# Decay attention and two gated MLPs: at most three loads of SyncE's queue under way

## The chip, the core and the metric
The kernel runs on one core of a Trainium2 chip. The metric is the device time of one execution in microseconds. Three runs of the kernel before took 586.87 us in the median (585.73 to 587.20). The engines are named as in the profile: PE (TensorE), PEld (its weight loads), DVE (VectorE), ACT (ScalarE), POOL (GpSimd) and SP (SyncE, which here issues all loads and stores).

## The reference
Batch 2, 8 heads, 768 positions, 64 channels per head; then 1536 tokens of 512 channels.

```python
for b in range(nb):                       # blocks of 64 positions
    intra = (qb @ kb.T * Dmask) @ vb      # Dmask: powers of the head's lam, lower triangle
    inter = (qb * lam_pow) @ kv_state
    out[:, :, sl] = intra + inter
    kv_state = lam_block * kv_state + (kb * rev_pow).T @ vb
x = out as tokens x 512
x = (sigmoid(x @ w_gate) * (x @ w_val)) @ w_out            # d_ff 1536
h = x @ w_in;  out = where(h > 0, h, exp(min(h, 0)) - 1) @ w_out2   # d_ff 2048
```

## The kernel before, in words
The attention takes the sequence in six chunks of 128 positions (`NCH`). For chunk c the kernel loads `tin` (k and q with channels on partitions; "t" of `load`, two halves of 512 KB for chunks 0 to 2, one load of 1 MB for the others) and `nat` (k and v with positions on partitions; "k" and "v", 512 KB each). `scores(c)` multiplies k and q (tile `st`, read from `tin`), in two halves g; behind each half it multiplies the decayed k of the chunk before with v (also into the bank of `st`, read from `nat` and `kd`; called u here). DVE masks the scores into `pr`, the x products multiply `pr` with v, and the ql product adds what the state `sn` brings. `split_chunk` splits the result into a high and a low part for the matmuls in fp32r, each dense product being three matmuls.

The first gate and value weights of the first MLP are multiplied directly while the attention runs (`direct`, tiles that the profile calls `warm` and `direct` by the name of their bank). All later products of a weight group go over seven fast products (M1 to M7, a scheme that saves one product of eight) with sums of weights made by POOL and DVE. A weight group is loaded raw into one buffer `w64` of 1 MB; ACT and DVE restore the floats from it (`fetch`), so the next raw group can be loaded when DVE's last step has read the buffer. The out products accumulate 256 columns of d_ff at a time in `xu`.

Nothing is issued where it is written. All operations are recorded as `Op`, `hazards` finds which wait for which, and `run` plays them through with costs for each engine, a list scheduler that is tried with several rules; `issue` then emits the instructions in the order of the best of these plays. So each engine runs its own fixed list, and a new edge in the graph can move any instruction of any engine but keeps the dependences. For SP, `hazards` chains the DMAs in the order in which the program writes them, and `run` treats the successor in this chain as ready once SP has issued the DMA before, not once it has landed. An `Op` can have a `fence`: another operation for which its first instruction waits by a dependence made by hand (`add_manual_dep`). Before the change only the ql product has one.

All operations are issued from one line of the helper, L182 in the profile, so its rows are told apart by tiles.

Of the kernel before, what the change touches and what calls it, by code (L numbers as in the profile page):

```python
# [108 lines left out]


class Op:
    __slots__ = ("eng", "call", "reads", "writes", "gap", "took", "port", "table", "preds", "shape", "fence", "words")

    def __init__(self):
        self.fence, self.words = None, 0


class Engine:
# [9 lines left out]
class Work:  # L128
# [78 lines left out]
    def hazards(self):  # L207
        write, read, banks, tables = {}, {}, {}, {1: [], 2: []}
        holder, users, freed = {}, {}, {}
        queued = -1  # L210
        for k, op in enumerate(list(self.ops)):
            e = ENGINES.index(op.eng)
            before = set()
            for v in op.reads + op.writes:
                slot = v.buf.slot
                if holder.setdefault(slot, v.buf) is not v.buf:
                    holder[slot] = v.buf
                    gone = Op()
                    gone.eng, gone.call, gone.preds = None, lambda: None, sorted(users.pop(slot))
                    freed[slot] = len(self.ops)  # L220
                    self.ops.append(gone)
                users.setdefault(slot, set()).add(k)
                if slot in freed:
                    before.add(freed[slot])
            for views, writes in ((op.reads, False), (op.writes, True)):
                for v in views:
                    for h in v.halves:
                        at = (v.buf.slot, h)
                        if v.buf.psum:
                            by = banks.setdefault(at, ({}, []))  # L230
                            before.update(by[0].values())
                            before.update(x for f, x in by[1] if writes or f != e)
                            continue
                        if at not in write:
                            write[at] = np.full(WORDS, -1, np.int32)
                            read[at] = []
                        before.update(np.unique(write[at][v.ix]).tolist())
                        if writes:
                            before.update(x for x, words in read[at] if words[v.ix].any())
            for views, writes in ((op.reads, False), (op.writes, True)):  # L240
                for v in views:
                    for h in v.halves:
                        at = (v.buf.slot, h)
                        if v.buf.psum:
                            if writes:
                                banks[at] = ({e: k}, [])
                            else:
                                banks[at][1].append((e, k))
                        elif writes:
                            write[at][v.ix] = k  # L250
                            for x, words in read[at]:
                                words[v.ix] = False
                            read[at] = [r for r in read[at] if r[1].any()]
                        else:
                            words = np.zeros(WORDS, bool)
                            words[v.ix] = True
                            read[at].append((k, words))
            if op.table:
                before.update(tables[3 - op.table])
                tables[op.table].append(k)  # L260
            if op.fence:
                before.add(self.ops.index(op.fence))
            if op.eng == "sync":
                before.add(queued)
                queued = k
            before -= {-1, k}
            op.preds = sorted(before)

    def run(self, preds, key, backward=False, gate=None, stick=0, thrift=20000):
        ops = self.ops[::-1] if backward else self.ops  # L270
        n = len(ops)
# [6 lines left out]
        free = dict.fromkeys(ENGINES, 0.0)  # L278
        port = behind = 0.0
# [23 lines left out]
        for _ in range(sum(op.eng is not None for op in ops)):  # L303
            t, e = min((free[e] if ripe[e] else max(free[e], soon[e][0][0]), i, e)
                       for i, e in enumerate(ENGINES) if ripe[e] or soon[e])[::2]
            while soon[e] and soon[e][0][0] <= t:
                k = heapq.heappop(soon[e])[1]
                heapq.heappush(ripe[e], (key[k], k))
            rank, k = heapq.heappop(ripe[e])
            if e == "tensor" and stick and ops[k].shape != shape:  # L310
                like = min((x for x in ripe[e] if x[0] < rank + stick and ops[x[1]].shape == shape), default=None)
                if like:
                    ripe[e].remove(like)
                    heapq.heapify(ripe[e])
                    heapq.heappush(ripe[e], (rank, k))
                    k = like[1]
            if e == "tensor" and not backward and thrift and stall(ops[k], t) > 100:
                like = min((x for x in ripe[e] if x[0] < rank + thrift and not stall(ops[x[1]], t)), default=None,
                           key=lambda x: (ops[x[1]].words, x))
                if like:  # L320
                    ripe[e].remove(like)
                    heapq.heapify(ripe[e])
                    heapq.heappush(ripe[e], (rank, k))
                    k = like[1]
            op = ops[k]
            if e == "sync":
                late = 300 if queue < t + 2000 or t < 3000 else 1100
                queue = max(t + 2000, queue) + op.took
                free[e], end[k] = t + op.gap, queue + late
            elif e == "tensor":  # L330
                t += 60 if t > free[e] + 1 else 0
                t += self.SWITCH if op.shape != shape else 0
                shape = op.shape
                late = 0.0
                if not backward:
                    late = stall(op, t, True)
                    told += op.words
                free[e], end[k] = t + late + op.gap, t + late + op.took
            else:
                if op.table and op.table != table:  # L340
                    t, table = t + self.TABLE, op.table
                go = max(t, port, behind if e == "gpsimd" else 0) if op.port else t
                free[e], end[k] = go + op.gap, go + op.took
                if op.port:
                    port = free[e]
                    behind = end[k] + self.HANDOFF["gpsimd"] if e == "vector" else 0
            start[k] = t
            done = [k]
            while done:
                x = done.pop()  # L350
                for s in after[x]:
                    f = ops[s].eng
                    ready = free[e] if f == e and e in ("tensor", "sync") and x == k else end[x] + self.HANDOFF.get(f, 0)
                    at[s] = max(at[s], ready)
                    left[s] -= 1
                    if left[s]:
                        continue
                    if f is None:
                        start[s] = end[s] = at[s]
                        done.append(s)  # L360
                    else:
                        heapq.heappush(soon[f], (at[s], s))
# [40 lines left out]
def tile_decay_attention_two_mlps(  # L403
# [245 lines left out]
    def load(c, what="tvk"):  # L649
        if c in tin:  # L650
            pass
        elif c == 2:
            tin[c] = sb.tile([P, 2, 2, 2, 2, CH], F32, "xPh1", name="tin2")
            nat_of[c] = sb.tile([P, 2, 2, H, D], F32, "sig1", name="nat2")
        else:
            tin[c] = sb.tile([P, 2, 2, 2, 2, CH], F32, ("gh1", "gl1")[int(c in (1, 4))], name="tin")
        t = tin[c].rearrange("p g b q i n -> p (g b q i n)"), att[c, 0]
        n = nat_of[c].rearrange("p q b h e -> p (q b h e)"), att[c, 1]
        first, second = slice(0, 1024), slice(1024, 2048)
        for x in what:  # L660
            for (to, src), cols in {"t": ((t, first), (t, second)) if c < 3 else ((t, slice(0, 2048)),), "v": ((n, second),),
                                    "k": ((n, first),)}[x]:
                nc.sync.dma_start(out=to[:, cols], in_=src[:, cols])

    load(0, "tv")
# [27 lines left out]
    n = 1  # L693
# [338 lines left out]
```

## Time and profile before
| | |
|---|---|
| median of three runs | 586.87 us (585.73 to 587.20) |
| the profiled execution's own time | 586.36 us |
| its span, first to last instruction | 584.6 us |
| mean granted clock of PE | 0.997 |
| PE busy | 573.1 us, 98% |
| DVE, ACT, POOL busy | 387.1, 301.7, 312.3 us |
| loads and stores | 51.4 MB, 24.1% of the DMA engines' span |

The span is 1.8 us shorter than the time of the execution, which includes start and end. PE's records are pipelined and a matmul's end is modelled, so its busy share says when matmuls followed one another, not that each was at its best. Idle time of the other engines means little as long as PE has work.

### The profile page before, as it was taken

To read this page: it belongs to the slowest core of one execution; us is meant where nothing else is said; L and a number is where in the kernel's file an instruction comes from. 1 tells how busy PE (TensorE), PEld (TensorE's weight loads), DVE (VectorE), ACT (ScalarE), POOL (GpSimd) and SP (SyncE) were. 2 spreads that over 40 slices of the span, in tenths; PEclk is the share of its full clock that TensorE was granted. 3 is DMA by queue.
4 is the path that set the end of the run, shared out by engine and by line. 5 is a ranking of instruction groups with operands and counts; after the bars stand their busy time and mean duration, and the time that the engine had idled before them with its cause. 6 is when DMAs were issued, how large, how long until landed. Compare 5 with 4: busy or idle time off the path is not lost.

```text
span 584.6 us, 10090 instructions
## 1 busy us (share of the span) xinstructions
PE 573.1 (98%) x4020; PEld 492.1 (84%) x4022; DVE 387.1 (66%) x683; ACT 301.7 (52%) x586; POOL 312.3 (53%) x265
## 2 busy tenths in 40 slices
PE   6999999999999999999999999999999999999997
PEld 3888898888888888888899788888888888888886
DVE  5787753476475466456549975677767685868484
ACT  4794656532433424344147887764545464636160
POOL 0688779567457447567238883572626355461100
PEclk9899999999999999999999999999999999999999
DMA  8955212321111201311201203322203011120014
GB/s 311 358 200 218 75 73 81 137 73 72 73 54 60 103 21 73 123 73 62 84 1 74 73 0 105 114 72 73 72 10 135 1 74 72 73 72 1 0 38 179
DMA packets 9983, 52.03 MB, mean 89 GB/s; under 512 B 1232, under 2 KB 1488, under 8 KB 5200
## 3 DMA queue, kind: packets, MB, share of 16 engines
q1 hardware_dynamic: 9936, 51.39, 24.1%
q8 instruction: 31, 0.51, 0.4%
q14 instruction: 16, 0.13, 0.1%
HBM read 48.24 MB, written 3.15 MB: 88 GB/s over the span
## 4 chain that ended last, share of the span: by engine, by line
PE 91%; DVE 3%; DMA 2%; ACT 1%; issue 1%; POOL 1%; SPq 0%; DVEq 0%
PE xu L182 36%; PE st L182 33%; PE direct L182 10%; PE warm L182 10%; PE x L182 2%; DMA tin<-in_att 2%; DVE sums L182 1%; SPq L182 0%; DVE xu L182 0%; DVE w L182 0%; POOL x143l L182 0%; DVE sig L182 0%; DVE xt L182 0%; ACT sig L182 0%; ACT L182 0%
## 5 line engine op out<-in xcount | busy, mean ns | idle before, releaser
L182 PE MATMUL xu<-gh,woh 128*128 128x512 f32 (+1 forms) x306 | 119.7, 394 | 1.5 <-DVE xt L182 1.4
L182 PE MATMUL xu<-gl,woh 128*128 128x512 f32 (+1 forms) x306 | 119.4, 390 | 0.0
L182 PE MATMUL xu<-gh,wol 128*128 128x512 f32 (+1 forms) x306 | 118.9, 389 | 0.0
L182 DVE TENSOR_TENSOR acc<-xu,acc 128x512 f32<-128x512 f32 x120 | 81.6, 687 | 44.6 <-PE xu L182 44.1
L182 POOL TENSOR_TENSOR gl<-sig,gh 128x1024 fp32r<-128x1024 f32 (+1 forms) x38 | 73.6, 1945 | 53.4 <-ACT gh L182 25.1
L182 POOL TENSOR_TENSOR t<-w 128x256 f32<-128x256 f32 (+1 forms) x80 | 68.9, 887 | 57.4 <-DVE w L182 53.4
L182 POOL TENSOR_TENSOR l<-t,h 128x768 fp32r<-128x768 f32 (+1 forms) x38 | 61.1, 1615 | 21.6 <-ACT h L182 19.1
L182 PEld LDWEIGHTS xu<-gh,woh 128*128 128x128 f32 x306 | 57.5, 188 | 13.8 <-DVE xt L182 2.0
L182 POOL TENSOR_TENSOR wol<-w,woh 128x512 fp32r<-128x512 f32 x26 | 33.1, 1293 | 65.4 <-ACT woh L182 59.4
L182 ACT CAST gh<-sig 128x512 fp32r<-128x512 f32 (+1 forms) x58 | 45.0, 787 | 44.5 <-DVE sig L182 42.7
L182 PEld LDWEIGHTS xu<-gh,wol 128*128 128x128 f32 x306 | 57.5, 188 | 11.6
L182 PEld LDWEIGHTS xu<-gl,woh 128*128 128x128 f32 x306 | 57.6, 188 | 10.1
L182 DVE SCALAR_TENSOR_TENSOR w<-w,w 128x1024 uint32<-128x1024 uint32 x34 | 54.6, 1605 | 0.2
L182 DVE TENSOR_TENSOR wt<-st,wt 128x512 f32<-128x512 f32 (+1 forms) x57 | 32.0, 562 | 33.9 <-PE st L182 33.3
L182 ACT ACTIVATE w<-w 128x1024 f32<-128x1024 f32 x34 | 38.7, 1139 | 28.0 <-DMA w<-in_w_gate 15.2
L182 PE MATMUL st<-x143l,h 128*128 128x512 f32 (+1 forms) x150 | 51.8, 347 | 0.0
L182 PE MATMUL st<-x143h,h 128*128 128x512 f32 (+1 forms) x150 | 51.5, 348 | 0.0
L182 PE MATMUL st<-x143h,l 128*128 128x512 f32 (+1 forms) x150 | 51.2, 347 | 0.0
L182 ACT ACTIVATE sig<-st 128x512 f32<-128x512 f32 (+1 forms) x52 | 29.3, 566 | 42.2 <-PE st L182 25.8
L182 DVE TENSOR_SCALAR w<-w 128x1024 uint32<-128x1024 uint32 x34 | 27.8, 817 | 24.3 <-ACT w L182 21.8
L182 ACT CAST h<-t 128x512 fp32r<-128x512 f32 (+1 forms) x40 | 28.9, 728 | 18.2 <-POOL t L182 14.5
L182 ACT ACTIVATE sig<-sig 128x256 f32<-128x256 f32 (+1 forms) x68 | 34.1, 508 | 1.5
(179 smaller groups left out, 1382.0 us busy)
## 6 DMA issues: line engine op xcount, KB each, us to landing
w<-in_w_out SPq DMA_DIRECT2D x14, 1024.0 KB, 4.8
w<-in_w_in SPq DMA_DIRECT2D x8, 1024.0 KB, 4.7
nat<-in_att SPq DMA_DIRECT2D x12, 512.0 KB, 7.8
w<-in_w_gate SPq DMA_DIRECT2D x6, 1024.0 KB, 4.7
w<-in_w_val SPq DMA_DIRECT2D x6, 1024.0 KB, 4.9
tin<-in_att SPq DMA_DIRECT2D x6, 512.0 KB, 8.4
tin<-in_att SPq DMA_DIRECT2D x3, 1024.0 KB, 12.7
out_t<-o SPq DMA_DIRECT2D x11, 256.0 KB, 2.0
```

Of the source, the lines that this page charges most:

```text
L182: return [getattr(getattr(self.nc, eng), fn)(*(real(a) for a in args), **{k: real(a) for k, a in kw.items()})]
```

## The change: a wait for the third load ahead
Each DMA that SP issues is listed in `loads`. A load (an operation that writes a tile; stores to the output do not) that has three or more ahead of it gets an edge from the third one ahead, and that one as its fence. SP therefore doesn't issue a load before the third one ahead of it has landed. The chain of issue order stays. In `run` the successor in the chain is still ready at issue, while the new edge makes a load ready when the load that it waits for has ended (`near`). The entry "q" in `load` is not used by any call. The graph is then played anew, so the order on all engines comes out of another search.

```diff
     def hazards(self):
...
-        queued = -1
+        queued, loads = None, []
...
             if op.eng == "sync":
-                before.add(queued)
-                queued = k
+                op.prev = queued
+                before.update(loads[-1:])
+                if len(loads) >= 3 and op.writes:
+                    before.add(loads[-3])
+                    op.fence = self.ops[loads[-3]]
+                loads.append(k)
+                queued = op
...
-                    ready = free[e] if f == e and e in ("tensor", "sync") and x == k else end[x] + self.HANDOFF.get(f, 0)
+                    near = e == "tensor" or e == "sync" and (ops[s].prev is op or op.prev is ops[s])
+                    ready = free[e] if f == e and x == k and near else end[x] + self.HANDOFF.get(f, 0)
```

SP at the program's start, before and then after; `DMAHW0` to `DMAHW7` are the semaphores of landed DMAs, taken in turn, so the k-th DMA of SP signals the semaphore of k modulo 8:

```order
L182 DMA lam<-in_lam 128x12
L182 DMA tin<-in_att 128x1024 x2
L182 DMA nat<-in_att 128x1024
L182 DMA w_84<-in_w_gate 128x2048
L182 DMA nat<-in_att 128x1024
L182 DMA tin<-in_att 128x1024 x2
L182 DMA nat<-in_att 128x1024 [waits DMAHW0_49]
L182 DMA w_84<-in_w_val 128x2048 [waits DMAHW1_49,DMAHW4_49,DVE_49,Activation_49]
```

The same loads in the changed program:

```order
L182 DMA lam<-in_lam 128x12
L182 DMA tin<-in_att 128x1024 x2
L182 DMA nat<-in_att 128x1024 [waits DMAHW0_49]
L182 DMA w_105<-in_w_gate 128x2048 [waits DMAHW1_49]
L182 DMA nat<-in_att 128x1024 [waits DMAHW2_49]
L182 DMA tin<-in_att 128x1024 [waits DMAHW3_49]
L182 DMA tin<-in_att 128x1024 [waits DMAHW4_49]
L182 DMA nat<-in_att 128x1024 [waits DMAHW5_49]
L182 DMA w_105<-in_w_val 128x2048 [waits DMAHW6_49,DVE_49,Activation_49]
```

The sequence of loads is the same. Before, seven DMAs behind lam had no wait for a landing, or one for a DMA eight ahead; now each names the semaphore of the DMA three ahead.

PE in chunk 1, from the end of the scores' second half (`st<-tin`) on; `st<-nat,kd` is the u product and `warm<-x11` the direct gate product:

```order
 L182 MATMUL st<-tin 64x64 x4
-L182 MATMUL warm<-x11h,x143h_252 128x256 x2
-L182 MATMUL warm<-x11h,h_267 128x256 x2
-L182 MATMUL warm<-x11l,h_242 128x256 x2
-L182 MATMUL warm<-x11l,x143h_252 128x256 x4
-L182 MATMUL warm<-x11l,h_267 128x256 x2
-L182 MATMUL warm<-x11h,l_259 128x256 x2
-L182 MATMUL warm<-x11h,x143h_252 128x256
 L182 MATMUL st<-nat,kd 64x64 x8
+L182 MATMUL warm<-x11h,h_254 128x256 x2
+L182 MATMUL warm<-x11h,x143h_277 128x256 x4
```

The second u product stood behind 15 dense matmuls and now stands ahead of them; four more, which stood between the two halves of the scores, also come behind it.

PE at the end of the direct gate product, before and then after; `warm<-x11h,h_495` and `h_518` are the first matmuls of the direct value product, `st<-tin` behind the gate product the scores of chunk 3:

```order
L182 MATMUL direct<-x11h,l_259 128x256 x2
L182 MATMUL direct<-x11h,x143h_252 128x256 x4
L182 MATMUL direct<-x11h,l_357 128x256 x2
L182 MATMUL st<-nat,kd 64x64 x8
L182 MATMUL warm<-x11h,h_495 128x256 x2
```

The changed program at this place:

```order
L182 MATMUL direct<-x11h,l_274 128x256 x2
L182 MATMUL direct<-x11h,x143h_277 128x256 x4
L182 MATMUL direct<-x11h,l_374 128x256 x2
L182 MATMUL st<-tin 64x128
L182 MATMUL st<-tin 64x2x64
```

The first scores of chunk 3 now stand ahead of the direct value product. On DVE, the first step on the gate weights (`TENSOR_SCALAR w`) stood ahead of the first `x11l` and now stands behind it.

## Rows read from the trace of the kernel before
**Rows 1.** The page: busy us, share of the span and instructions of each engine.
```profile
PE 573.1 (98%) x4020; PEld 492.1 (84%) x4022; DVE 387.1 (66%) x683; ACT 301.7 (52%) x586; POOL 312.3 (53%) x265
```
**Rows 2.** Stretches: length, PE, PEld, DVE, ACT, POOL busy; clock, DMA share, GB/s.
```profile
12.00:14.70 2.70, 0.00 (x0) 0.00 (x0) 2.54 (x4) 2.70 (x9) 0.00 (x0) 1.00 1.03 413
16.10:19.40 3.30, 3.30 (x45) 2.84 (x42) 3.30 (x9) 2.86 (x8) 2.56 (x3) 0.50 0.90 356
...
80.00:300.00 220.00, 220.00 (x1222) 191.45 (x1221) 126.62 (x204) 88.96 (x151) 129.70 (x111) 1.00 0.21 75
```
**Rows 3.** PE's waits: us in total, times, longest us.
```profile
PE st L182 <- DMA tin<-in_att: 2.9, 1, 2.9
PE xu L182 <- DVE xt L182: 1.4, 2, 1.2
...
PE direct L182 <- ACT sig L182: 0.5, 1, 0.5
...
PE direct L182 <- ACT wt L182: 0.5, 1, 0.5
```
**Rows 4.** SP in order of time: start us, us, the loads that it issues.
```profile
2.58 0.52 SPq L182 DMA_DIRECT2D w<-in_w_gate  x1
...
3.87 1.06 SPq L182 DMA_DIRECT2D tin<-in_att  x2
...
14.65 0.33 SPq L182 DMA_DIRECT2D w<-in_w_val  x1
...
15.50 1.16 SPq L182 DMA_DIRECT2D tin<-in_att  x2
...
17.78 0.38 SPq L182 DMA_DIRECT2D tin<-in_att  x1
```
**Rows 5.** Loads issued at 1.16, 2.58, 3.87, 3.87, 16, 17.78, 43.28: KB, us to landing.
```profile
tin<-in_att SPq DMA_DIRECT2D x1, 512.0 KB, 4.1
...
w<-in_w_gate SPq DMA_DIRECT2D x1, 1024.0 KB, 8.4
...
tin<-in_att SPq DMA_DIRECT2D x1, 512.0 KB, 10.9
...
tin<-in_att SPq DMA_DIRECT2D x2, 512.0 KB, 11.2
...
tin<-in_att SPq DMA_DIRECT2D x1, 512.0 KB, 9.5
...
tin<-in_att SPq DMA_DIRECT2D x1, 1024.0 KB, 12.7
...
tin<-in_att SPq DMA_DIRECT2D x1, 1024.0 KB, 4.9
```
**Rows 6.** PE in order of time: start us, us, tiles, shapes, count [idle before].
```profile
14.77 0.90 PE L182 MATMUL st<-tin 64*64 64x128 f32 x32 [2.85 <-DMA tin<-in_att]
...
17.49 1.56 PE L182 MATMUL st<-tin 64*64 64x128 f32 x32
...
21.16 0.69 PE L182 MATMUL st<-nat,kd 128*64 128x64 f32 x16
...
22.72 1.67 PE L182 MATMUL x<-pr,nat 64*64 64x64 f32 x48
...
24.64 1.10 PE L182 MATMUL x<-ql,sn 64*64 64x128 f32 x32
...
28.89 0.50 PE L182 MATMUL direct<-x11l,h 128*128 128x256 f32 x2
...
29.71 0.40 PE L182 MATMUL direct<-x11l,h 128*128 128x256 f32 x2
...
32.37 0.51 PE L182 MATMUL warm<-x11h,h 128*128 128x256 f32 x2
...
330.36 0.50 PE L182 MATMUL xu<-gh,woh 128*128 128x512 f32 x1 [1.17 <-DVE xt L182]
```
**Rows 7.** DVE in order of time: the first x11l.
```profile
12.77 0.68 DVE L182 TENSOR_TENSOR x11l<-x,x11h 128x512 fp32r<-128x512 f32 x1
```

More of the change, by code (lines that the diff above doesn't have):

```diff
@@ L111 @@
 class Op:
-    __slots__ = ("eng", "call", "reads", "writes", "gap", "took", "port", "table", "preds", "shape", "fence", "words")
+    __slots__ = ("eng", "call", "reads", "writes", "gap", "took", "port", "table", "preds", "shape", "fence", "words", "prev")
     def __init__(self):
-        self.fence, self.words = None, 0
+        self.fence, self.words, self.prev = None, 0, None
 class Engine:
@@ L660, in load @@
         for x in what:
-            for (to, src), cols in {"t": ((t, first), (t, second)) if c < 3 else ((t, slice(0, 2048)),), "v": ((n, second),),
-                                    "k": ((n, first),)}[x]:
+            for (to, src), cols in {"t": ((t, first), (t, second)) if c < 3 else ((t, slice(0, 2048)),), "q": ((t, second),),
+                                    "v": ((n, second),), "k": ((n, first),)}[x]:
                 nc.sync.dma_start(out=to[:, cols], in_=src[:, cols])
```

## The prediction
> **What bounds the kernel now.** I read the page's busy times first: PE is busy for 573.1 of the 584.6 us of the span, the next engine for 387 [rows 1]. The stretches tell the same without an average: from 80 to 300 us PE works for 220.00 of 220.00 us [rows 2]. The reader should see that there is nothing to win in such a stretch except by taking work from PE, and the change takes none away. So I looked for the places where PE does not work, in its waits: 2.9 us once for a load of tin, 1.4 us for DVE's xt, 0.5 us each for ACT's sig and wt [rows 3]. The load's wait ends at 14.77 us, when the first scores of chunk 1 begin [rows 6]. Behind it the granted clock is 0.50, the lower of its two levels of 1.2 and 2.4 GHz, from 16.10 to 19.40 us; PE had stood still from 12.00 to 14.70 [rows 2]. The 3.3 us at half clock cost up to 1.65 us. All of this lies in the first 33 us, where SP has many loads under way: at 2.58 us it issues w_gate and at 3.87 the two loads of tin for chunk 1 [rows 4], when only lam can have landed. Once the attention's data is in, only weights are left, and their single raw buffer lets one load be under way at a time.
>
> **Part 1: what the new waits do to the loads.** SP's order of loads stays; only the time of issue moves. The question is whether a load is still issued early enough to start when those ahead of it are done. Unqueued, 512 KB land 4.1 us and 1 MB 4.9 us after issue [rows 5]. In the queue's full stretch the core moves 413 GB/s [rows 2], so 512 KB take 1.27 us, 1 MB 2.54, and the fixed part of a load is some 4.9 - 2.54 = 2.4 us (4.1 - 1.27 = 2.8 at the start of the program). Two loads of 512 KB in front cover 2.54 us of it, or one of 1 MB alone. So the cap of three is just enough where three loads go round, and too little only by the time in which the slowest part of a load lags. Walking through it:
> - w_gate waits for the first load of tin (1.16 + 4.1 = 5.3 us instead of an issue at 2.58). The queue ahead of it is busy to about 8, and 5.3 + 2.4 = 7.7: no change. It lands at 2.58 + 8.4 = 11.0 as before.
> - the first half of tin for chunk 1 waits for the first nat of chunk 0, which lies one w_gate ahead of 11.0, at about 8.5; it was issued at 3.87 and landed 10.9 later, at 14.77. With w_gate and another nat still ahead of it, an issue at 8.5 changes nothing. PE's 2.85 us stay, and so does the half clock behind them.
> - the second half waits for w_gate (11.0), starts by 13.4 at the earliest and lands at about 16, where it landed before (the two took 11.2 in the median, so this one 11.5, from about 4.4).
> - w_val was issued at 14.65, bound by DVE's read of the raw weights, not by a load. In the new order DVE makes an x11l (0.68 us) ahead of the first step on w [rows 7], which pushes w_val to about 15.3, and all loads behind it by 0.65.
> - the load of tin for chunk 3 was issued at 17.78 and landed 12.7 later, at 30.5. Now it must wait for the second load of tin for chunk 2, which landed at 16.0 + 9.5 = 25.5 and will land at 26.1. From 26.2 it needs at least 4.9: 31.1, and with the 0.65 in front and a gap in the queue of up to 1, 31.5 to 32 [rows 4, 5].
> The weight loads behind the attention never have three under way, because of their one buffer: no cost.
> What stands against this in the Trainium skill, in "DMA: Bandwidth & Descriptors", section "Rules for kernel authors": a DMA should be issued early and waited for late, since then its fixed cost overlaps; the same page fits that fixed cost at about 2.0 us. By that rule every load that is now held back would lose cover, up to those 2.0 us each time as an estimate from that page; this is the rival B below, whose price is from rows. The trace agrees on the fixed part (2.4 us by rows), and has it covered by the transfers of the other two.
>
> **Part 2: what the new order does on PE.** The waits enter the planner's graph, and the order of all engines but SP is a new one. To the start of the first ql product (24.64 us before) I add up the new order. Scores of chunk 1, first half: 0.85, from 14.77 to 15.6. Their u product: 0.7, to 16.3. The second half comes right behind now and runs at half clock, 1.56 us as in its row, to 17.85; its u product takes 0.69 at full clock and about 1.2 here, to 19.05. Then 18 dense matmuls of 256 columns in one go, 0.12 each by the spacing of their rows and some at half clock: 2.4, to 21.45. The x products take 1.67 as at 22.72, two more dense ones 0.35 with the change of tile: 23.47. Before, three dense matmuls more were done by then (0.35), so the lead is 24.64 - 0.35 - 23.47 = 0.8 us [rows 6]. It comes from the u product, which stood at 21.16 behind 15 dense matmuls and held DVE's pr of the second half, since both use one bank; it now stands ahead of them.
> From there: ql product about 0.9, one dense, scores of chunk 2 0.85, u 0.69, three dense, scores 0.85, u 0.69, and 24 dense matmuls at 0.12 with four changes of tile: PE is through with the direct gate product at about 31.1. Then the new order asks for the first scores of chunk 3, which before stood behind the first direct products of w_val (these began at 32.37 [rows 6]). tin lands at 31.5 to 32: PE waits 0.4 to 0.9, I take 0.6. ACT's pieces of w_val come at about 32.4 by the durations of its casts in its new order, so this wait is partly one that ACT would impose anyway. By 32.5 to 32.8 the direct w_val product starts as before, with 0.85 us of scores done ahead: lead 0.4 to 0.7; I take 0.7 with the bounds 0 and 1.6.
> After that, up to the end of the attention, PE's list has 38 runs of one kind in the new order against 33 (counted in the order). A change of tile costs 0.10: the pair of dense matmuls behind one takes 0.50, others 0.40 [rows 6]. Five more: +0.5.
> The rest of the order holds the same matmuls (1650 of 512 columns, 1284 of 256). What its new waits cost no row can tell: at best the waits for sig, wt and xt are gone (-0.5 - 0.5 - 1.4 = -2.4), at worst there are as many again (+2.4). At the change of layers, where the 1.17 us before 330.36 are [rows 6], the units stand about as close to one another as before, so I take 0.
> **Sum.** -0.7 + 0.5 + 0 = -0.2 on the profiled execution's 586.36 us (span 584.6 and 1.8 around it): 586.2. The median of the three runs, 586.87, is 0.5 above that execution; I give 586.4, between the two. No difference under 0.3% (1.8 us) can be told from no change here.
>
> **Rivals.**
> A, faster: the new order closes waits beyond the first 33 us. For it: the attention's work is spread more evenly between the direct and the first fast products, just where sig and wt held PE, so 1.0 may go; if xt's 1.4 goes too: 586.4 - 2.4 = 584.0, and 583.2 with the upper bound of the start. Against it: more changes of tile, and a change of layers that looks alike.
> B, slower: the cap leaves the queue dry. Place: the loads from w_val to tin of chunk 3. A load's landing counts when its slowest part is in; the first tin load of chunk 1 landed at 14.77, 1.3 us later than w_gate's 11.0 and the 1 MB behind it call for (11.0 + 2.4 = 13.4), and each round of three that waits for such a late part loses up to 2 us. One lost round makes PE wait 2.0 us longer at 31 us, and the clock may fall behind it as behind the 2.85 us: 1.65 more. 586.4 + 3.65 = 590.0. It decides from the point where SP issues tin of chunk 3 after 28.5 us instead of 26.2. Against it: the transfers of two loads cover the 2.4 us.
> C, slower: new waits on PE at the end of the attention or the change of layers, as many again as now: 586.4 + 2.4 = 588.8.
> D, the cap does nothing: the order of SP shows the waits on the semaphores of the third load ahead, so it is there; that it moves no landing that PE waits for is the forecast's own first half, and the time is then the new order's alone, 585.6 to 586.4.
>
> **Numbers.** Forecast with D 0.46, own range 584.7 to 588.1; A 0.28; B 0.15; C 0.11. So faster 0.28, same 0.46, slower 0.26. The range goes to 583.4, most of A, and to 589.5, C and part of B.
>
> **What would show it.** Right: PE's wait for tin still ends at 14.7 to 14.9 us with the clock at 0.50 behind it; w_val is issued near 15.3, tin of chunk 3 near 26.2; PE has one more wait for tin, 0.4 to 0.9 us near 31; the first ql product starts about 1 us earlier; PE's busy time stays at 573 within 1. Wrong: a second stretch at half clock; a wait of 2 us for a load; PE's idle time outside the first 33 us changed by more than 2 us.

## The result and the profile after

The changed kernel took 590.98 us in the median of five runs (589.80 to 592.95), the kernel before 585.73 us in five runs beside it (585.39 to 587.20): ratio 1.0089, 95% interval [1.0074, 1.0104]. It is slower by about 5.2 us, outside the predicted range of 583.4 to 589.5 us. The profiled execution took 590.91 us, its span is 589.1 us.

The page of the changed kernel: busy us, share and instructions, then the granted clock of PE and the GB/s in 40 slices of 14.7 us.

```profile
PE 576.8 (98%) x4020; PEld 495.3 (84%) x4022; DVE 392.7 (67%) x683; ACT 302.0 (51%) x586; POOL 313.1 (53%) x265
...
PEclk9889999999999999999999999999999999999999
...
GB/s 287 281 293 160 131 73 72 86 63 71 139 0 72 144 1 72 142 20 54 143 2 72 71 1 83 72 133 70 73 29 55 62 144 0 72 71 1 0 37 178
```

PE has as many instructions as in [rows 1] and is busy 3.7 us longer. Some of that is a lower clock, which shows in the third slice (29 to 44 us; the second was at 8 before as well); some is the new order's own, as the experiment without waits tells below. The stretches tell where (length, PE, PEld, DVE, ACT, POOL busy; clock, DMA share, GB/s):

```profile
15.00:33.00 18.00, 16.77 (x336) 14.79 (x328) 11.89 (x23) 13.24 (x36) 12.11 (x10) 0.91 0.88 299
33.00:60.00 27.00, 25.63 (x552) 23.26 (x552) 19.81 (x51) 17.26 (x48) 20.94 (x16) 0.94 0.63 214
...
80.00:300.00 220.00, 219.88 (x1211) 191.51 (x1210) 126.36 (x199) 88.68 (x152) 130.95 (x113) 1.00 0.22 77
...
15.40:18.78 3.38, 3.38 (x71) 3.03 (x65) 2.60 (x7) 2.85 (x10) 2.92 (x3) 0.50 0.99 299
35.84:39.26 3.42, 3.42 (x18) 3.42 (x18) 3.28 (x7) 3.37 (x11) 3.42 (x4) 0.50 0.82 259
```

From 80 to 300 us PE's busy time is that of [rows 2] to 0.12 us. The half clock at 15.4 is the one of before, half a microsecond earlier; the one at 35.84 is new. From 15 to 33 us the loads move 299 GB/s. The same stretch of the kernel before:

```profile
15.00:33.00 18.00, 17.46 (x341) 15.66 (x334) 12.90 (x27) 14.72 (x40) 12.14 (x11) 0.91 0.98 372
```

PE's waits after, in total, times and longest, answer to [rows 3]:

```profile
PE st L182 <- DMA tin<-in_att: 6.0, 3, 3.5
```

One wait of 2.9 us has become three. PE in order of time, answering to [rows 6]:

```profile
14.71 1.00 PE L182 MATMUL st<-tin 64*64 64x128 f32 x32 [3.45 <-DMA tin<-in_att]
...
23.54 1.10 PE L182 MATMUL x<-ql,sn 64*64 64x128 f32 x32
...
27.20 0.90 PE L182 MATMUL st<-tin 64*64 64x128 f32 x32 [0.20 <-DMA tin<-in_att]
...
31.57 0.40 PE L182 MATMUL direct<-x11h,l 128*128 128x256 f32 x2
34.37 0.90 PE L182 MATMUL st<-tin 64*64 64x128 f32 x32 [2.40 <-DMA tin<-in_att]
...
36.99 1.05 PE L182 MATMUL warm<-x11l,x143l 128*128 128x256 f32 x4
```

The reader should see a good start (ql at 23.54 instead of 24.64), a wait of 2.40 us for tin of chunk 3, and behind it dense matmuls at half clock: 1.05 us for four that take 0.64 elsewhere. SP in order of time, answering to [rows 4], and the loads' median us from issue to landing in the first 60 us, answering to [rows 5]:

```profile
5.38 0.33 SPq L182 DMA_DIRECT2D w<-in_w_gate  x1
...
13.29 0.33 SPq L182 DMA_DIRECT2D nat<-in_att  x1
14.76 0.33 SPq L182 DMA_DIRECT2D w<-in_w_val  x1
15.94 0.33 SPq L182 DMA_DIRECT2D nat<-in_att  x1
19.23 3.46 SPq L182 DMA_DIRECT2D tin<-in_att  x2
23.64 1.60 SPq L182 DMA_DIRECT2D nat<-in_att  x2
27.22 0.33 SPq L182 DMA_DIRECT2D tin<-in_att  x1
```

```profile
nat<-in_att SPq DMA_DIRECT2D x12, 512.0 KB, 6.0
tin<-in_att SPq DMA_DIRECT2D x6, 512.0 KB, 5.3
...
w<-in_w_val SPq DMA_DIRECT2D x1, 1024.0 KB, 7.6
```

The attention's loads of 512 KB now take less time from issue to landing (6.0 and 5.3 us in the median, where the page before has 7.8 and 8.4), since fewer stand ahead of them, and yet from w_val on they land later; w_val itself takes 7.6 us instead of 5.1. A load's landing is recorded in sixteen parts, and who waits is released by the last. Before, w_val had landed at 19.7 us, the second tin of chunk 2 at 25.5, tin of chunk 3 at 30.5, and nat of chunk 4's k at 38.3. After, it is 22.4, 27.2, 34.2 and 44.4. From the exact times the delays are 2.6, 1.7, 3.7 and 6.0 us: not larger with every load, but largest at the end of the queue.

### The profile page after: what moved, and what is told of

Its sections match the earlier page's. It is cut to its first block, busy times and chain, and to the rows that moved or that the text cites. A ratio compares the mean times of both kernels' runs of the same rounds, so it can differ in the third digit from the quotient of the medians.

```text
span 589.1 us, 10095 instructions
## 1 busy us (share of the span) xinstructions
PE 576.8 (98%) x4020; PEld 495.3 (84%) x4022; DVE 392.7 (67%) x683; ACT 302.0 (51%) x586; POOL 313.1 (53%) x265
## 4 chain that ended last, share of the span: by engine, by line
PE 82%; DMA 6%; DVE 4%; POOL 3%; ACT 3%; issue 1%; SPq 0%; DVEq 0%; POOLq 0%; ACTq 0%
PE xu L182 33%; PE st L182 30%; PE direct L182 9%; PE warm L182 9%; DMA tin<-in_att 3%; PE x L182 2%; DVE w L182 2%; POOL gl L182 1%; DMA w<-in_w_val 1%; DMA nat<-in_att 1%; ACT w L182 1%; POOL l L182 1%; DMA w<-in_w_in 1%; DVE sums L182 1%; POOL t L182 1%
## 5 line engine op out<-in xcount | busy, mean ns | idle before, releaser
L182 PEld LDWEIGHTS xu<-gl,woh 128*128 128x128 f32 x306 | 57.6, 188 | 11.3 <-POOL gl L182 1.2
L182 ACT CAST h<-t 128x512 fp32r<-128x512 f32 (+1 forms) x40 | 28.8, 726 | 14.3 <-POOL t L182 13.2
L182 ACT ACTIVATE sig<-sig 128x256 f32<-128x256 f32 (+1 forms) x68 | 34.5, 508 | 1.4
```

The lines of the kernel that those rows point to most:

```text
L182: return [getattr(getattr(self.nc, eng), fn)(*(real(a) for a in args), **{k: real(a) for k, a in kw.items()})]
```

## The experiments

My theory after the result: each round of three loads loses a little, because the third is released by the slowest part of the first and then needs its own fixed time and its own slowest part; the losses add up until PE waits at 34 us. The rivals: the new order of the engines costs the 5 us; one wait (that of tin of chunk 3) costs them; the half clock behind the new wait costs them. The kernel before took 585.69 to 585.95 us in the median beside these runs.

### The waits without the new order, and the order without the waits

`e1_old_order_cap3` has the order of the kernel before on every engine and the waits of the change:

```diff
+                if len(loads) >= 3 and op.writes:
+                    op.cap = self.ops[loads[-3]]
+                loads.append(k)
...
+                for m in made[op.cap][-4:] if op.cap else ():
+                    tc.add_manual_dep(made[op][0].ins, m.ins.name, behind, reason="third load ahead")
```

> The order of all engines as in the kernel before; only SP's waits for the third load ahead are added. Theory W (the waits thin the queue, and the new order asks for tin of chunk 3 too early for that): the loads land as late as in the changed kernel (tin of chunk 3 near 34.2 us), but the old order asks for that tin only at 35.5, so no wait there and no half clock near 36; the scores of chunk 2 may wait some 1 us for the second half of tin (landing 27 instead of 25.5). 586.5 to 588.5 us, ratio to before 1.001 to 1.005. Rival O (the new order alone costs the time, the waits nothing): the same time as before, ratio 0.998 to 1.002, and tin of chunk 3 lands near 30.5.

595.0 us, ratio 1.0148 [1.0127, 1.0170]. PE's waits to 60 us, and one row of ACT:

```profile
PE st L182 <- DMA tin<-in_att: 4.7, 2, 4.1
PE x L182 <- DVE sums L182: 2.3, 1, 2.3
```

```profile
46.47 2.16 ACT L182 ACTIVATE kd<-nat,low 128x128 f32<-128x128 f32 x7 [3.87 <-DMA nat<-in_att]
```

`e2_new_order_no_waits` has the order of the changed kernel and the waits gone again:

```diff
-                for m in made[op.fence][-4:] if op.fence else ():
+                for m in made[op.fence][-4:] if op.fence and op.eng != "sync" else ():
```

> The order of the changed kernel, without the waits for the third load ahead. Theory W: tin of chunk 3 lands near 31, before PE asks for it at about 31.9; no wait of 2.4 us, no half clock near 36; 585 to 587 us, ratio to before 0.997 to 1.003. Rival O: 590 to 591 us, ratio 1.008 as in the changed kernel, with the waits spread elsewhere in the attention.

586.78 us, 1.0012 [1.0000, 1.0024]. PE on its page, and PE's waits:

```profile
PE 574.9 (98%) x4022; PEld 493.6 (84%) x4022; DVE 393.4 (67%) x683; ACT 301.5 (52%) x586; POOL 313.0 (54%) x265
```

```profile
PE st L182 <- DMA tin<-in_att: 3.4, 1, 3.4
...
PE xu L182 <- POOL gl L182: 0.8, 1, 0.8
PE warm L182 <- ACT sig L182: 0.5, 1, 0.5
```

My theory W asked for 586.5 to 588.5 us in e1; it looked at tin of chunks 2 and 3. PE does not wait for tin of chunk 3 there, as I had said, but in other places: 1.3 us longer for tin of chunk 1 (4.1 instead of 2.9) and 2.3 us for DVE's sums. e2 came out as expected.

The waits cost 9.2 us in the old order; the new order alone costs 1.0, with an interval that begins at no difference; both together cost 5.2. So the waits are the loss, and the search that knows of them wins back some 4 us of it. In e1 it is also ACT that stands still: its casts for PE stand behind `kd`, which waits for a nat.

### How many loads under way are enough

`e3_new_order_cap5` waits for the fifth load ahead in the changed kernel's order, `e5_old_order_cap4` for the fourth in the order before, `e4_cap4_planned` is the change itself with four instead of three, planned anew, and `e10_new_order_cap2` the changed kernel's order with the second. In e3 and e10 the edge for the planner stays at three, so that the order does:

```diff
-                    op.fence = self.ops[loads[-3]]
+                    op.cap = self.ops[loads[-5]] if len(loads) >= 5 else None
```

> The order of the changed kernel, with waits for the fifth load ahead instead of the third. Theory W: five under way keep the queue fed while the slowest part of a load lags; tin of chunk 3 lands 31 to 32, PE waits under 0.5 us; time within 0.2% of the run without waits. Rival O: 590 to 591 us. A third theory (each wait of SP costs by itself, whatever the depth): as in the changed kernel, 590 us, with as many waits.

> The order of the kernel before, with waits for the fourth load ahead instead of the third, which cost 9.2 us there. Theory L (the wait is for a load's slowest part, which lags 2 to 3 us once instruction fetches of PE share a DMA engine; two loads in flight don't cover the lag and the fixed 2.4 us, three nearly do): most of the loss goes, 586 to 588 us. Rival F (the fixed time of a load alone, uncovered by bytes in flight): three loads of 512 KB are 3.8 us of transfer against 2.4, so nothing is left, 585.5 to 586.3. Rival S (each wait on SP costs by itself): 594 to 595 us.

> The change with four loads under way instead of three, planned anew. Theory W: its order asks for the loads much like the changed kernel's, and the queue runs dry less: tin of chunk 3 about 1 to 2 us earlier than 34.2, so the wait at chunk 3 is 0.5 to 1.5 us; 587 to 589 us. Rival O: as the changed kernel, 590 to 591.

> The changed kernel's order on every engine, with each load of SP waiting for the second one ahead instead of the third. Theory (a round of n loads takes its transfer, 1.27 us for 0.52 MB, the fixed 2.4 us and a lag of some 1.6 us for the slowest part): two loads of 0.52 MB in 5.3 us, 200 GB/s from 15 to 33 us (190 to 215 with the 1 MB loads in between), tin of chunk 3 lands after 40 us, and the time is above 597. Rival (no lag, only the fixed part): 2 x 0.52 MB in 3.67 us, 285 GB/s, tin of chunk 3 at 35 to 36, 592 to 594. If what slows the loads were something else than the waits, the rate would stay at 299.

The same stretch in e10, and then in e5 and e3:

```profile
15.00:33.00 18.00, 13.11 (x264) 11.73 (x264) 9.73 (x17) 11.69 (x34) 9.68 (x8) 0.80 0.70 237
```

```profile
15.00:33.00 18.00, 18.00 (x347) 16.39 (x340) 12.86 (x27) 14.57 (x39) 12.09 (x11) 0.91 0.96 358
```

```profile
15.00:33.00 18.00, 18.00 (x369) 16.18 (x362) 13.84 (x27) 14.99 (x41) 12.72 (x11) 0.91 0.96 377
```

| at most under way | GB/s, 15 to 33 us | time, us | ratio |
|---|---|---|---|
| 2, new order (e10) | 237 | 602.08 | 1.0280 [1.0260, 1.0301] |
| 3, new order (changed kernel) | 299 | 590.98 | 1.0089 [1.0074, 1.0104] |
| 3, old order (e1) | 266 | 595.00 | 1.0148 [1.0127, 1.0170] |
| 4, old order (e5) | 358 | 586.84 | 1.0023 [1.0005, 1.0041] |
| 4, planned anew (e4) | 355 | 588.67 | 1.0045 [1.0032, 1.0058] |
| 5, new order (e3) | 377 | 586.93 | 1.0015 [1.0002, 1.0027] |
| no such waits, new order (e2) | 374 | 586.78 | 1.0012 [1.0000, 1.0024] |

With the same rule for every load, the rate rises with the number under way until it meets the queue's own at four to five. e3 has nearly as many waits of SP as the changed kernel and costs nothing over e2, so the theory that each wait costs by itself falls. e5's 586.84 us lie in the range of theory L; its interval also reaches that of rival F, so this run doesn't part the two.

A round of three in the changed kernel takes 3 x 0.524 MB (512 KB) / 299 GB/s = 5.3 us. The transfer of one load (1.27) and the fixed part (2.4) make 3.7, so each round loses about 1.6 us more. With two it is 2 x 0.524 / 237 = 4.4 us, 0.75 over the 3.7. So the loss per round is not a constant. My expectation for e10 carried the 1.6 over, and its 190 to 215 GB/s was too low; its rival without a lag (285) was too high, and its time of 592 to 594 is excluded. Both rounds are averages, with the 1 MB load of w_val in the stretch.

Nor is all of the loss an empty queue: the busy share of the DMA engines in this stretch is 0.98 before, 0.88 in the changed kernel and 0.70 in e10, and the rate over that share falls too (372 / 0.98 = 380, 299 / 0.88 = 340, 237 / 0.70 = 339 GB/s). With fewer loads under way the packets also take longer for the same bytes; why, no run shows.

In e4 tin of chunk 3 lands at 30.8, as without waits, and yet its median is 1.8 us above that of e5 (the intervals of the two ratios overlap a little): its own order brings waits of 1.4 us for ACT's low and 0.8 for DVE's sums. My theory for e4, an earlier tin and a shorter wait for it, had the range right (587 to 589 us) and not the cause. A new search can cost as much as a wait.

### Which waits

`e6_late_waits` keeps the waits only from w_val on, `e7_early_waits` only ahead of w_val, `e12_one_wait` only that of tin of chunk 3:

```diff
+                    op.cap = self.ops[loads[-3]] if len(loads) >= 9 else None     # e6
+                    op.cap = self.ops[loads[-3]] if len(loads) < 9 else None      # e7
+                    op.cap = self.ops[loads[-3]] if len(loads) == 15 else None    # e12
```

> The order of the changed kernel, with the waits for the third load ahead only from w_val on; the first loads as before. Theory L: tin of chunk 3 is late as in the changed kernel (33.5 to 34.5 us), the wait of about 2 us and the half clock behind it stay: 589.5 to 591 us. Rival E (the early waits start the lateness): 587 us or less.

> The order of the changed kernel, with the waits for the third load ahead only up to the last load of chunk 1; none from w_val on. Theory L: the queue refills by itself, tin of chunk 3 lands 31 to 32 us, no second half clock: 586.5 to 587.5 us, as without any of these waits. Rival E: 590 us.

> The changed kernel's order on every engine, and of all the new waits only one: the load of tin for chunk 3 waits for the second load of tin for chunk 2. Theory (one wait costs about what the prediction gave it; the 4 us that tin of chunk 3 lost add up over the rounds before it): with no waits ahead, tin of chunk 2 lands at 25.4 and tin of chunk 3 is issued there instead of near 18; it lands at 31 to 32.3 (30.4 without any wait, 34.2 with all), and by 1.1 us of time for each us that it lands later (the slope of the runs with this order so far) the time is 587.5 to 588.8. Rival (this one wait is the whole loss): it lands after 33.5 and the time is above 590. If the time does not go by this landing, it is that of the order without waits, 586.8.

e6 took 589.32 us (1.0069 [1.0047, 1.0092]), e7 588.57 (1.0047 [1.0032, 1.0063]). Over e2 that is 2.5 and 1.8 us, together 4.3, where the changed kernel has 4.2: the two halves add, as far as intervals of about 1 us each can tell. In e6 tin of chunk 3 landed at 32.4, earlier than theory L had it (33.5 to 34.5), and the time is just under its range. I had expected less of e7 (586.5 to 587.5), because its loads behind w_val are free to run ahead; but what its first nine loads lost was not caught up: w_val landed at 23.2 and tin of chunk 3 at 32.1.

e12 took 587.33 us (1.0022 [1.0005, 1.0039]), 0.55 over e2, a difference that the two intervals don't show to be real. It lies below the 587.5 to 588.8 that I had given it. SP in e12, and its PE's waits for loads:

```profile
16.71 0.97 SPq L182 DMA_DIRECT2D nat<-in_att  x2
25.59 0.33 SPq L182 DMA_DIRECT2D tin<-in_att  x1
```

```profile
PE st L182 <- DMA tin<-in_att: 3.4, 1, 3.4
```

```profile
15.00:33.00 18.00, 18.00 (x373) 16.18 (x364) 13.82 (x27) 15.28 (x41) 12.78 (x11) 0.91 0.87 309
```

The load is issued at 25.59 instead of 17.72 (in e2), 7.9 us later, and lands at 30.6 instead of 30.4. One wait for the third load ahead, in a queue that is full at that moment, costs that load 0.2 us. The same load in the changed kernel is issued 1.6 us later still, at 27.22, and lands 3.6 us later, at 34.2: 7.0 us from issue instead of 5.0, because the two nats ahead of it were held back as well: they land 2.4 and 4.1 us behind its issue, in e12 1.2 and 2.5 us. In both it lands 2.6 to 2.9 us behind the second of them. So the rival of the one wait falls.

The last row warns against the rate of a fixed stretch: e12 moves 309 GB/s in it, little more than the changed kernel, because the loads behind this one come later, and pays at most little for it. What counts is the landing that PE waits for.

### The half clock

`e9_fill_second_wait` is the changed kernel with 20 matmuls more, whose product nothing uses, right ahead of the scores of chunk 3; `e8_idle_fill` is the kernel before with 12 such ahead of those of chunk 1:

```diff
+                for _ in range(20 if op.pad else 0):
+                    out, w, x = (v.ap() for v in op.pad)
+                    self.nc.tensor.matmul(out, lhsT=w, rhs=x, start=True, stop=True)
```

> The kernel before, with 12 more matmuls on the idle tile right before the scores of chunk 1, where PE waits 2.85 us for tin; they add no result. If the clock falls because PE stands still there, it stays at 2.4 GHz from 16 to 19.4 us, and up to 1.65 us come back: 584 to 585.3 us, ratio 0.997 to 0.999. If the clock falls for another reason, or if PE is held by other things in those 3.4 us: 585.5 to 586.5 us.

> The changed kernel with 20 more matmuls of 256 columns on PE right ahead of the first scores of chunk 3, into the bank that those scores then overwrite; their product is used by nothing. By their spacing of 0.12 us they take 2.4 us, the length of PE's wait for tin there. Theory (the wait is paid once as 2.4 us and again as the half clock behind it, 35.84 to 39.26, up to 1.7 us): the clock stays at 2.4 GHz there, and the time falls by 1 to 1.7 us to 589.3 to 590. Rival (behind the wait ACT and the attention's chain hold PE, as they did when idle matmuls kept the clock up before the scores of chunk 1): the clock stays up as well, new waits for ACT or DVE of 1 to 2 us come behind it, and the time is 590.5 to 591.2. If the matmuls are no cover for the clock, the stretch at half clock stays and the time is 591.

e8 took 585.6 us, 1.0000 [0.9987, 1.0014]. The stretch of the half clock in it, and a wait that it did not have before:

```profile
16.10:19.40 3.30, 3.30 (x51) 2.97 (x51) 3.30 (x9) 2.97 (x9) 2.58 (x2) 1.00 0.94 371
```

```profile
PE warm L182 <- ACT sig L182: 1.8, 1, 1.8
```

The clock stays up, PE is through its list earlier and waits 1.8 us for ACT instead. So my theory was right on the clock and not on the 584 to 585.3 us. Executions without fillers say the same: of the 73 executions of the kernel before that stand beside the experiments, 20 had a mean clock of at least 0.999 and took 585.4 us in the median, 41 had 0.996 or 0.997, as one stretch of 3.4 us at half clock makes it, and took 585.7. So the half clock of the start costs some 0.2 us at the end, as far as this comparison can tell, and not 1.65. The 12 with 0.993 or 0.994, two such stretches or one twice as long, took 587.0: more of it does cost something.

e9 took 591.89 us, 1.0107 [1.0090, 1.0125], 0.9 over the changed kernel and above both of my ranges. PE and ACT in e9, and after it the ql product and the same ACT row of the changed kernel:

```profile
32.95 2.56 PE L399 MATMUL st<-x11h 128*128 128x256 f32 x20
35.44 0.90 PE L182 MATMUL st<-tin 64*64 64x128 f32 x32
...
43.76 1.10 PE L182 MATMUL x<-ql,sn 64*64 64x128 f32 x32
...
49.78 0.45 PE L182 MATMUL x<-pr,nat 64*64 64x64 f32 x12 [0.33 <-DVE x22l L182]
```

```profile
45.48 1.28 ACT L182 ACTIVATE kd<-nat,low 128x128 f32<-128x128 f32 x4 [1.75 <-DMA nat<-in_att]
```

```profile
44.18 1.10 PE L182 MATMUL x<-ql,sn 64*64 64x128 f32 x32
```

```profile
44.44 1.28 ACT L182 ACTIVATE kd<-nat,low 128x128 f32<-128x128 f32 x4 [0.28 <-DMA nat<-in_att]
```

The clock stays up behind the filled wait (no half level between 21 and 60 us). From the scores of chunk 3 to the ql product e9 needs 43.76 - 35.44 = 8.3 us, the changed kernel 44.18 - 34.37 = 9.8 us: the half clock is worth 1.5 us in that stretch. Then it is gone: nat of chunk 4's k lands at 45.4 in e9 and 44.4 in the changed kernel, ACT waits for it in front of the casts of chunk 3's result, DVE's x22l and then PE's x product come 0.75 us later than in the changed kernel, though PE had been 0.42 ahead. So the second half clock need not add its 1.7 us to the end; the next late load can take them back. In the changed kernel itself ACT already waits 0.28 us for this nat, so an earlier PE would have met the same landing. e9 alone doesn't prove it: that its loads land about 1 us later than the changed kernel's, and that its first stretch at half clock is twice as long (14.3 to 21.1), I can't explain, and its time holds the cost of both. Of the five executions of the changed kernel four had a mean clock of 0.994 and one 0.997, thus one stretch less; it took 590.98 us, the median of the five. That is one execution, so how much the second half clock costs stays open between 0 and its 1.7 us.

### Could the start be had for less

`e11_tin_ahead_of_gate` is the kernel before, without waits, with tin of chunk 1 loaded ahead of w_gate and planned anew:

```diff
-    load(1, "t")
...
-    load(1, "tv")
+    load(1, "v")
```

(the load of chunk 1's tin now stands in front of that of w_gate).

> The kernel before, without the new waits, with the load of tin for chunk 1 written ahead of that of w_gate and nat of chunk 0's k behind it, and planned anew. Theory (PE's start is set by whichever of the loads, ACT's restored gate weights and the attention's chain comes last): PE's wait of 2.85 us for tin at 14.7 us goes or shrinks under 1 us, w_gate lands 2 to 3 us later, ACT's pieces and with them the direct gate product come later, PE waits for ACT instead: 584.5 to 587, no clear gain. Rival (the wait for tin and the half clock behind it are what the start loses): 582 to 584.

588.9 us, 1.0056 [1.0040, 1.0073]: slower, and above both ranges. Its PE's waits:

```profile
PE st L182 <- ACT kd L182: 3.0, 1, 3.0
PE st L182 <- DMA tin<-in_att: 1.5, 2, 1.3
```

The wait of 2.85 us for tin moved to ACT's kd at the same place, and the half clock (16.7 to 20.1) with it. No version here beats the kernel before.

### The time goes with one landing

All kernels with the new order, by the landing of tin of chunk 3:

| kernel | landed, us | time, us |
|---|---|---|
| e3, e2 | 30.3, 30.4 | 586.93, 586.78 |
| e12 | 30.6 | 587.33 |
| e7 | 32.1 | 588.57 |
| e6 | 32.4 | 589.32 |
| changed kernel | 34.2 | 590.98 |
| e9 | 35.2 | 591.89 |
| e10 | 42.9 | 602.08 |

A microsecond of landing costs 4.2 / 3.8 = 1.1 us from e2 to the changed kernel and 15.3 / 12.5 = 1.2 from e2 to e10. This landing stands for a queue that is late as a whole; in e12 only the loads behind it are late (nat of chunk 4's k at 40.8 instead of 38.1), and the 0.55 us there are within the noise. The slope holds for this one order: e4, with another, is at 588.67 with a landing at 30.8.

## Why the prediction was wrong

- **The step that failed** is in part 1: "So the cap of three is just enough where three loads go round, and too little only by the time in which the slowest part of a load lags." I named that lag, priced it once in rival B and left it out of the walk, but for "a gap in the queue of up to 1" at its end. What a round of three takes beyond transfer and fixed part measures about 1.6 us on the average, and it falls due round after round, so the stretch ran at 299 GB/s instead of 372. Runs show the loss per round; that it is the slowest part of a load is my reading, since the sixteen parts spread over 1.8 to 3.1 us there, and no run varied this spread by itself.
- **The walk itself.** Right up to chunk 1: tin's first half was to land as before (the wait ended at 14.71), its second at about 16 (15.9), the half clock was to stay. w_val was to be issued at 15.3, since DVE's x11l was put in front; it was 14.76, released by the landing of tin's first half at 14.67 and no longer by DVE, which was done at 14.3; so that delay did not arise. What I did not walk through were the landings behind it: nat of chunk 1 waited for a nat whose last part came 2.0 us behind its first, and landed at 19.2 instead of 17.2; w_val took 7.6 us instead of 5.1 (5.0 in e12) and landed 2.6 late. For tin of chunk 3 I gave an issue at 26.2 and 4.9 us from there, with 31.5 to 32 as its landing; it was 27.22 and 7.0, and 34.2. The 4.9 is the row of a load in an empty queue; e12 shows that it holds (5.0) when the two loads ahead land within 2.5 us of the issue. In the closed chain of three the second took 4.1.
- **PE's wait** was taken as 0.6 us and was 2.40, with 0.20 more in chunk 2. The waits for tin are 6.0 us instead of the 3.4 of e2: 2.6 more. With half of the 3.42 us at half clock that makes 4.3, which agrees with the 4.2 between the two medians; but how much of the half clock reaches the end is not shown: in e9 it was gone and the time was not less.
- **Part 2.** The lead of 0.8 us at the first ql product was right: 24.64 - 0.35 - 23.54 = 0.75. The whole order's -0.2 was +1.0 by the medians of e2 (0.0 to 1.4 by the ratio's interval), inside what I could tell from no change. PE's busy time was to stay at 573 within 1. In e2 the waits for xt and wt of [rows 3] are gone, as in the best case that I had named, but PE is busy 574.9 us: the order that waits less has the same matmuls take 1.8 us longer, where I had given 0.5 for five changes of tile.
- **Rival B** had the mechanism (a queue left dry between w_val and tin of chunk 3, one longer wait, a second half clock) and, with 590.0, nearly the time; I gave it 0.15. Its argument against itself, that the transfers of two loads cover the 2.4 us, was the failed step again. Its 2.0 us longer wait was an estimate for one lost round, and PE's wait of 2.40 us is what several rounds added up to, so the nearness of the two is in part luck. Its point of decision was wrong as well: it was to hold only if SP issued tin of chunk 3 after 28.5, and it held at 27.22, because the load then took 7.0 us. The rule of the Trainium skill that I set against the change ("DMA: Bandwidth & Descriptors", "Rules for kernel authors": issue early, wait late) pointed the right way; the table of loads under way agrees with it, and e12 bounds it: one load issued 7.9 us later landed 0.2 us later, with the queue ahead of it full. The 2.0 us that I took from the same page of the Trainium skill (section "Anatomy of one DMA") are its fit for DMAs that GpSimd issues; here SyncE issues all loads, and the rows give 2.4.
- **Rival A** had two of the waits right that would go (in e2 xt's and wt's are gone, 0.5 us for sig is left), and not that PE pays for them in busy time. **Rival C** did not happen: from 80 to 300 us the two profiles agree, and the change of layers brings no new wait over 0.8 us. **Rival D** fell: the cap moved landings that PE waits for.

## What to carry to other kernels

How many loads must be under way is the rate wanted times the whole round, from a load's landing to the landing of the one it released, and the round is longer than transfer and fixed time alone (here 5.3 us with three loads and 4.4 with two, instead of 3.7); read it from a chain of loads that wait for one another, not from a lone load. Where the chain is closed, a small loss per round adds up over the rounds, so walk it load by load to the first one that somebody waits for. And before pricing a lost clock or a wait on the busiest engine at its full length, look for the next thing that arrives late: filling either wait with idle matmuls kept the clock up behind it, and the end moved not at all in one case and the wrong way in the other, where later loads had a part in it.

## What the runs showed of the hardware

The sixteen parts of a load land within 0.4 to 0.5 us of each other for the first four loads after lam in the changed kernel. A block of instructions (one packet of 16 KB) is fetched at 12.1 us for 0.9 us, the first of this size in the trace; the nat that lands across it spreads over 2.0 us (11.3 to 13.3), and those to 34 us over 1.8 to 3.1. In e10, with two loads under way, the spread is 0.8 to 1.0 us for the three loads that land between 16 and 21 us, and 3.8 us for w_val, whose landing begins at 23.0, behind the fetch at 22.7. In the kernel before the picture is cleaner: such a fetch takes 1.0 us from 12.15 and another from 22.61, and in the loads that land behind each (tin at 14.72, tin at 25.46) fifteen parts come within 0.9 us and only the last is 1.2 and 1.4 us behind; between them, once the loads ahead of w_val were through, the last part is at most 0.4 us behind. So a late sixteenth of a load may come from the fetches. They can't be all of it: of w_val in the changed kernel four parts come 1 us or more behind the other twelve. No run moved the fetches, and the cause stays open. Nor is the spread the work of the change: before, it costs little, because the loads behind are issued already.

The clock fell to 0.50 behind PE's wait of 2.4 us, and not behind the filled one; how much was lost could only be told from what stood behind it. It does not fall behind every such wait: in e6 PE waits 2.9 us before the scores of chunk 1 as in the kernel before, and the clock stays at 1.00 from 15 to 33 us.

```profile
PE st L182 <- DMA tin<-in_att: 5.1, 3, 2.9
```

```profile
15.00:33.00 18.00, 15.79 (x357) 14.04 (x353) 12.91 (x25) 14.33 (x38) 12.28 (x10) 1.00 0.89 307
```
